# Attention then SwiGLU on one core: weights loaded between x and the last rows, and a new order of the opening steps

## The chip, the cores and the metric

The kernel runs on one core of a Trainium2 chip. The metric is the device time of one execution in microseconds (us); less is better. The core has five engines that run side by side, each through its own list of instructions in order: TensorE (PE, matrix products), VectorE (DVE), ScalarE (ACT), GpSimd (POOL) and SyncE (SP, which here only issues the DMA transfers). An instruction waits for semaphores of the instructions whose results it reads or whose buffers it overwrites, and whatever stands behind it on its engine waits too.

## The reference

```
def mab(q, kv):                              # x: 4 x 12416 x 128, inducing: 32 x 128
    s = scale * (q @ kv.transpose(0, 2, 1))
    s = s - s.max(-1, keepdims=True)
    a = np.exp(s)
    a /= a.sum(-1, keepdims=True) + 1e-09
    return a @ kv
h = mab(I, x)                                # 32 rows gather from all of x
y = mab(x, h)                                # each row of x reads the 32 rows of h
g = y @ w_gate                               # 128 x 1536
out = (g / (1 + np.exp(-g)) * (y @ w_val)) @ w_out   # 1536 x 128
```

The three weights arrive as 64-bit floats and x as 32-bit floats.

## The kernel before

A batch has 12416 rows; a "slot" is one of 12 slices of the hidden width (1536 = 12 x 128) for one tile of up to 512 rows, and a batch has 300 slots. In a slot PE makes a gate product and a value product (`front`, lines 694 and 695), ACT the silu (`gate`), DVE the product of both (`value`), ACT or DVE a rounded copy h_hi and POOL or DVE the rest h_lo (`split`), and PE adds three products with the output weights (`back`, lines 737 to 739). The attention of the next batch is woven into the slots. Only the first batch has nothing to be woven into, so the kernel opens with a prologue whose order is written out by hand in two tables of tokens, START and SECOND; the list of every engine follows the order of the tokens.

The prologue of batch 0 goes as follows. Seven chunks of x (14 blocks of 128 rows each, the last 13) are loaded with the channels on partitions. Each chunk gets scores (`s1`) and their maximum, an exponential (`e1`), a transposition of the exponentials on DVE (`eT`), and a sum over the rows weighted by them (`hq`, 2 PE rows per block). `hq` needs x with rows on partitions, which comes either from a second load (`ln`) or by turning blocks on PE with a copy out of PSUM on DVE or ACT (`tx`). Chunks 0 to 3 share one maximum and 4 to 6 another (`mb`); `hb` and `hc` join the two halves into h, and `hd` turns it (hT, hTs).

Each weight piece is 128 x 512 numbers of 64 bits, 512 KB: J0 to J5 for the gate and value weights (a piece serves two slots), o0 to o2 for the output weights (a piece serves four). It is converted to 32 bits by integer steps: `X` (scale the high words) and `low` (scale the low words) on ACT, `sh` and `jn` on DVE (lines 190 and 193), `add` on POOL (line 196). Then the J pieces are multiplied by hT (`pa`, line 402), because the gate product works on attention weights and not on y, and are rounded in ACT and DVE steps (`pk`, `pb`, `pm`, `pc`). The o pieces are split into wo_hi (`hi`, ACT) and wo_lo (`lo`, POOL).

The first tile of 512 rows is served in its own short way (`z0` to `z8`): scores against hTs, maximum, exponential, sum, division, and a spread into `stack`, which `front` reads. In SECOND `f`, `g`, `m`, `k` are front, silu, value and back of the 12 slots of this tile; `back` uses the 32-bit weights whole for it (`u.whole`, line 734). Slots 0 to 11 are this tile; slot 12 opens the loop, when seven of the tile's twelve backs are done and five are pending; the loop takes one back per slot.

```
if u.whole:
    k = t % (WP // P)
    nc.tensor.matmul(out=o[:, :n], lhsT=pieces[f"o{t // (WP // P)}"].w[:, P * k:P * k + P], rhs=u.h[:, :n], ...)
```

Of the kernel before, what the change touches and what calls it, by code (L numbers as in the profile page):

```python
# [9 lines left out]
F32 = mybir.dt.float32  # L10
# [8 lines left out]
P = 128  # L19
# [9 lines left out]
def starts(sizes):  # L29
# [46 lines left out]
low:o0 X:o0 sh:J2 X:J3 sb:4:20:0 z6:0 z7:0 jn:J2 pk:0 z6:1 z7:1 z8:0 pb:0 pa:1 z8:1 sh:o0 sh:J3 e2:4:20 add:J2 jn:o0 pk:1 f:0 pm:1 sl g:0 pc:1 f:1
jn:J3 pa:2 f:2 g:1 add:o0 m:0 pk:2 X:J4 sum:1 f:3 pm:2 add:J3 rec:1 m:1 g:2 X:o1 k:0 pa:3 pc:2 g:3 low:J4 sh:J4 m:2 f:4 f:5 jn:J4 k:1 pk:3 sh:o1 g:4
m:3 no:1:1 pm:3 k:2 at:1 X:J5 sh:J5 pc:3 g:5 low:J5 jn:J5 low:o1 jn:o1 add:J4 pa:4 add:J5 f:6 m:4 pk:4 m:5 g:6 pb:4 k:3 f:7 pa:5 m:6 add:o1 ah:1:1 f:8
al:1:0 g:7 X:o2 pk:5 sh:o2 g:8 low:o2 k:4 pm:5 f:9 jn:o2 pc:5 k:5 f:10 sp:1 m:7 k:6 m:8 f:11 g:9 add:o2 m:9 g:10 g:11 m:10 m:11 hi:o0 lo:o0 hi:o1
lo:o1  # L80
# [3 lines left out]
    13: "hi:o2",  # L84
    14: "lo:o2",
# [26 lines left out]
def induced_set_attention_then_swiglu(ctx: ExitStack, tc: tile.TileContext, xt, xn, ind, wgv, wo, out):  # L112
# [58 lines left out]
    class Piece:  # L171


        def __init__(self, work, k, i):
            self.k, self.i = k, i
# [7 lines left out]
        def low(self):  # L183
            nc.scalar.activation(out=self.lw.bitcast(I32), in_=self.lw, func=AF.Copy, scale=2.0 ** -29)  # L184
# [684 lines left out]
```

## Time and profile before

| what | value |
|---|---|
| runs (3) | 1376.89, 1376.9, 1377.32 us; median 1376.9 |
| span of the profiled execution, first to last instruction | 1374.8 us |
| PE busy in the span | 1366.1 us (99%) |
| ACT, DVE, POOL busy | 91%, 87%, 86% |
| DMA traffic | 119.49 MB, mean 87 GB/s |

The profile is of one execution. Its span is 2.1 us under the median of the runs, the part of a run that lies outside its first and last instruction. A busy share is a mean over stages: PE is bound from the loop on, while the prologue's 55 us have other limits, so the prologue is read by stages.

### The profile page before, as it was taken

The numbers are of one execution on the slowest core, as the hardware profiler recorded it, in microseconds if no ns is written. First come the engines' busy times: TensorE is split into PE (matmuls) and PEld (weight loads), VectorE is DVE, ScalarE is ACT, GpSimd is POOL, SyncE is SP. The second block draws the span as 40 slices with busy tenths as digits, with TensorE's granted clock in tenths as the row PEclk, the third lists the DMA queues.
The fourth block names the chain that finished last, engine by engine and source line by source line (L and its number), as shares of the span: only waits on it lengthen the run. The fifth ranks groups of instructions, "written<-read, shape, count | busy, mean of one in ns | idle before, by whom it ended". The sixth has DMA issues, their size and how long they took to land.

```text
span 1374.8 us, 25215 instructions
## 1 busy us (share of the span) xinstructions
PE 1366.1 (99%) x7459; PEld 1183.8 (86%) x7459; DVE 1195.4 (87%) x2088; ACT 1245.7 (91%) x2380; POOL 1179.8 (86%) x994
## 2 busy tenths in 40 slices
PE   9999999999999999999999999999999999999998
PEld 6578788889988887899998888789999888889998
DVE  6899879998988889898898888988888888888887
ACT  4989898889998887999999889799999999999998
POOL 1689878989988878899899878889989989989987
PEclk9999999999999999999999999999999999999999
DMA  9234433312144243221123522321111111111110
GB/s 370 81 96 133 160 104 114 119 56 71 38 130 160 94 143 112 67 62 37 44 72 119 192 80 95 123 73 52 44 38 45 39 47 39 39 46 38 43 44 22
DMA packets 50680, 119.49 MB, mean 87 GB/s; under 512 B 11376, under 2 KB 28272, under 8 KB 50544
## 3 DMA queue, kind: packets, MB, share of 16 engines
q1 hardware_dynamic: 50544, 117.90, 26.3%
q8 instruction: 59, 0.97, 0.3%
q14 instruction: 77, 0.63, 0.2%
HBM read 62.54 MB, written 25.43 MB: 64 GB/s over the span
## 4 chain that ended last, share of the span: by engine, by line
PE 97%; ACT 1%; DMA 1%; DVE 1%; issue 0%; SPq 0%; DVEq 0%
PE o L737 18%; PE gv L694 18%; PE gv L695 18%; PE o L738 18%; PE o L739 18%; PE gv L275 2%; PE o L323 1%; PE o L275 1%; DMA xt_sb<-xt 1%; PE o L734 0%; ACT silu L700 0%; PE gv L424 0%; PE gv L267 0%; ACT xn_sb L184 0%; DVE eT L313 0%
## 5 line engine op out<-in xcount | busy, mean ns | idle before, releaser
L718 POOL TENSOR_TENSOR h_lo<-h,h_hi 128x512 fp32r<-128x512 f32 (+1 forms) x889 | 1088.6, 1250 | 147.7 <-ACT h_hi L716 104.7
L700 ACT ACTIVATE silu<-gv 128x512 f32<-128x512 f32 (+1 forms) x1200 | 704.8, 589 | 95.5 <-PE gv L694 69.9
L708 DVE TENSOR_TENSOR h<-gv,silu 128x512 f32<-128x512 f32 (+1 forms) x891 | 590.9, 669 | 90.5 <-PE o L738 50.7
L716 ACT CAST h_hi<-h 128x512 fp32r<-128x512 f32 (+1 forms) x778 | 468.9, 603 | 0.8 <-DVE h L708 0.8
L694 PE MATMUL gv<-stack,tw 128*128 128x512 f32 (+1 forms) x1200 | 452.7, 377 | 1.3 <-DVE stack L544 1.0
L695 PE MATMUL gv<-stack,tw 128*128 128x512 f32 (+1 forms) x1200 | 448.2, 374 | 0.0
L737 PE MATMUL o<-h_hi,wo_lo 128*128 128x512 f32 (+1 forms) x1188 | 445.6, 375 | 0.0
L739 PE MATMUL o<-h_lo,wo_hi 128*128 128x512 f32 (+1 forms) x1188 | 443.2, 373 | 0.0
L738 PE MATMUL o<-h_hi,wo_hi 128*128 128x512 f32 (+1 forms) x1188 | 443.2, 373 | 0.0
L708 DVE TENSOR_TENSOR gv<-gv,silu 128x512 f32<-128x512 f32 (+1 forms) x297 | 201.5, 678 | 66.0 <-PE o L738 46.0
L694 PEld LDWEIGHTS gv<-stack,tw 128*128 128x128 f32 x1200 | 227.0, 189 | 33.9 <-ACT tw L416 3.0
L737 PEld LDWEIGHTS o<-h_hi,wo_lo 128*128 128x128 f32 x1188 | 224.8, 189 | 33.4 <-issue 10.6
L695 PEld LDWEIGHTS gv<-stack,tw 128*128 128x128 f32 x1200 | 227.0, 189 | 28.0 <-ACT silu L700 1.6
L739 PEld LDWEIGHTS o<-h_lo,wo_hi 128*128 128x128 f32 x1188 | 224.8, 189 | 24.3 <-POOL h_lo L718 0.3
L738 PEld LDWEIGHTS o<-h_hi,wo_hi 128*128 128x128 f32 x1188 | 224.8, 189 | 23.2
L718 DVE TENSOR_TENSOR h_lo<-gv,h_hi 128x512 fp32r<-128x512 f32 (+1 forms) x297 | 197.6, 665 | 0.8
L716 ACT CAST h_hi<-gv 128x512 fp32r<-128x512 f32 (+1 forms) x295 | 168.8, 572 | 10.1 <-DVE gv L708 8.4
L211 DVE TENSOR_REDUCE h_hi<-h 128x512 fp32r<-128x512 f32 (+1 forms) x113 | 73.7, 661 | 0.0
L748 DVE COPY ob<-o 128x512 f32<-128x512 f32 (+1 forms) x99 | 65.8, 665 | 0.2 <-PE o L739 0.2
L484 POOL TENSOR_TENSOR a_lo<-aT,a_hi 128x480 fp32r<-128x480 f32 (+2 forms) x26 | 29.9, 1151 | 0.0
L196 POOL TENSOR_TENSOR wgv_sb<-s_all 128x512 int32<-128x512 int32 x2 | 2.9, 1487 | 28.4 <-ACT s_all L184 28.4
L471 POOL TENSOR_TENSOR s_all<-s_all,sm 128x512 f32<-128x512 f32 (+2 forms) x27 | 26.1, 966 | 0.0
(156 smaller groups left out, 480.2 us busy)
## 6 DMA issues: line engine op xcount, KB each, us to landing
xt_sb<-xt SPq DMA_DIRECT2D x32, 896.0 KB, 5.1
xn_sb<-xn SPq DMA_DIRECT2D x18, 896.0 KB, 6.1
out<-ob SPq DMA_DIRECT2D x52, 256.0 KB, 2.0
out<-ob SPq DMA_DIRECT2D x48, 240.0 KB, 2.0
stack<-a_hi SPq DMA_DIRECT2D x96, 64.0 KB, 2.0
stack<-a_lo SPq DMA_DIRECT2D x96, 64.0 KB, 2.0
stack<-a_hi SPq DMA_DIRECT2D x96, 60.0 KB, 2.0
stack<-a_lo SPq DMA_DIRECT2D x96, 60.0 KB, 2.0
```

Source lines behind the costliest of these rows:

```text
L211: nc.vector.tensor_reduce(out=out, in_=in_.unsqueeze(2), op=ALU.max, axis=AX.X)
L275: nc.tensor.matmul(out=ps[32 * j:32 * j + 32, 32 * (lo - b0):32 * (hi - b0)], lhsT=lhsT, rhs=st.xt[q][:, lo - CH0[q]:hi - CH0[q], j, :], s ...
L694: nc.tensor.matmul(out=u.g[:, :n], lhsT=st.w[:, wcol(0, t)], rhs=rhs, start=True, stop=True)
L695: nc.tensor.matmul(out=u.v[:, :n], lhsT=st.w[:, wcol(1, t)], rhs=rhs, start=True, stop=True)
L700: nc.scalar.activation(out=u.s[:, :u.n], in_=u.g[:, :u.n], func=AF.Silu)
L708: nc.vector.tensor_mul(out=u.h[:, :n], in0=u.v[:, :n], in1=u.s[:, :n])
L716: u.cast(out=u.hi[:, :n], in_=u.h[:, :n])
L718: eng.tensor_sub(out=u.lo[:, :n], in0=u.h[:, :n], in1=u.hi[:, :n].bitcast(F32))
L737: nc.tensor.matmul(out=o[:, :n], lhsT=wo_lo[:, ws], rhs=hi, start=(t == 0), stop=False)
L738: nc.tensor.matmul(out=o[:, :n], lhsT=wo_hi[:, ws], rhs=hi, start=False, stop=False)
L739: nc.tensor.matmul(out=o[:, :n], lhsT=wo_hi[:, ws], rhs=lo, start=False, stop=(t == NT - 1))
L748: (nc.scalar.copy if u.last else nc.vector.tensor_copy)(out=ob[:, :n], in_=o[:, :n])
```

## The change

Both tables are written anew, and steps that were one token are parted so that PE's half and the reader's half can stand apart (`tp`/`te`, `s1p`/`s1e`, `mbp`/`mbe`, `ha0`/`hap`/`har`, `hdp`/`hds`/`hdt`, `fg`/`fv`).

- Loads: the chunks of x come in the order 0, 3, 2, 1, 5, 4, 6; then J1, o1, o0, J3, J2, J0; then the rows of chunk 6; then J4, J5, o2. Chunks 0 to 5 are turned on PE whole (84 blocks; before 61, with chunks 4, 5 and two thirds of 6 loaded a second time).
- Weights are joined in place: `t` of a J piece is its place in wgv_sb. `X` and `low` of J1, o1, o0 and `X` of J3 and o2, `low` of J5, run on POOL. Six of the nine pieces have their `sh`, and five their `jn`, ahead of `hc`.
- The first tile takes the split weights like all others (three fp32r products per back; `u.whole` is gone), so its h is split too, its first ten casts (`c`) and ten remainders (`l`) in SECOND.
- `pm` and `pc` go for all pieces; the first tile's scores use the layout of the others with a DVE transposition (`z0t`); four groups of PE transposes whose result is not used (`wm`, 5 + 5 + 3 + 10 blocks behind the first 9) go; `hi` and `lo` of o2 move from slots 13 and 14 into the first tile.

```
-lx:0:0:4 lx:0:4:14 lx:1 lx:2 lx:3 lx:4 lx:5 lx:6 ln:4 ln:5 ln:6:0:8 ld:J0:s0 ld:J1:s1 ld:J2:t0 ld:J3:t1 wm:9
+lx:0:0:4 lx:0:4:14 lx:3 wm:9 tp:0:0 te:0:0:1 lx:2 tp:0:1 tp:0:3 te:0:1:0 s1p:0 te:0:3:1 tp:0:2 s1e:0 lx:1 ...
-            self.t = work[:, 2 * WP:3 * WP].bitcast(U32)
             self.w = work[:, 2 * WP:3 * WP] if k == "o" else wgv_sb[:, self.cs]
+            self.t = self.w.bitcast(U32)
...
-        def X(self):
-            nc.scalar.activation(out=self.t.bitcast(F32), in_=self.hw.bitcast(F32), func=AF.Copy, scale=2.0 ** -112)
+        def X(self, e=0):
+            if e:
+                nc.gpsimd.tensor_scalar(out=self.t.bitcast(F32), in0=self.hw.bitcast(F32), scalar1=2.0 ** -112, scalar2=None, op0=ALU.mult)
+            else:
+                nc.scalar.activation(out=self.t.bitcast(F32), in_=self.hw.bitcast(F32), func=AF.Copy, scale=2.0 ** -112)
...
-        if u.whole:
-            k = t % (WP // P)
-            nc.tensor.matmul(out=o[:, :n], lhsT=pieces[f"o{t // (WP // P)}"].w[:, P * k:P * k + P], rhs=u.h[:, :n], start=(t == 0), stop=(t == NT - 1))
-        else:
-            hi, lo = turns(u.hi[:, :n]), turns(u.lo[:, :n])
...
+        hi, lo = turns(u.hi[:, :n]), turns(u.lo[:, :n])
+        nc.tensor.matmul(out=o[:, :n], lhsT=wo_lo[:, ws], rhs=hi, start=(t == 0), stop=False)
+        nc.tensor.matmul(out=o[:, :n], lhsT=wo_hi[:, ws], rhs=hi, start=False, stop=False)
+        nc.tensor.matmul(out=o[:, :n], lhsT=wo_hi[:, ws], rhs=lo, start=False, stop=(t == NT - 1))
```

**DVE, the last steps ahead of `hc`.** Before, between the second maximum and `hc` (L384), DVE has the transpositions eT and small steps of the join alone:

```order
L313 STREAM_TRANSPOSE eT<-s_all 128x448 x2
L313 STREAM_TRANSPOSE eT<-s_all 128x416
L354 TENSOR_REDUCE fac<-sum_262 128x1
L357 TENSOR_TENSOR fac<-fac 128x2
L361 TENSOR_REDUCE r_445<-gv 128x1
L362 TENSOR_SCALAR r_445<-r_445 128x1
L363 RECIPROCAL r_445<-r_445 128x1
L364 TENSOR_SCALAR fac<-fac,r_445 128x2
L381 TENSOR_SCALAR hn<-o,fac 128x128
L384 SCALAR_TENSOR_TENSOR hn<-o,fac,hn 128x128
```

In the changed kernel the same stretch (here from the second half's `ha0` on, L381; `hc` is L416, `sh` L196, `jn` L199) reads:

```order
L381 TENSOR_TENSOR fac<-fac 128x2
L196 TENSOR_SCALAR wgv_sb<-wgv_sb 128x512
L331 STREAM_TRANSPOSE eT<-s_all 128x448
L389 TENSOR_REDUCE r_456<-gv 128x1
L390 TENSOR_SCALAR r_456<-r_456 128x1
L391 RECIPROCAL r_456<-r_456 128x1
L392 TENSOR_SCALAR fac<-fac,r_456 128x2
L196 TENSOR_SCALAR wgv_sb<-wgv_sb 128x512
L413 TENSOR_SCALAR hn<-o,fac 128x128
L331 STREAM_TRANSPOSE eT<-s_all 128x416
L199 SCALAR_TENSOR_TENSOR wgv_sb<-tw,wgv_sb 128x512 x2
L196 TENSOR_SCALAR wgv_sb<-wgv_sb 128x512
```

Weight steps now stand between the small ones, and two `jn` and a `sh` between the last eT and `hc`, which is the next row. Three more `sh` and three `jn` stand ahead of this piece.

**POOL, its first work after the constants.** Before it is the adds, from J0 on:

```order
L196 TENSOR_TENSOR wgv_sb<-s_all 128x512 x2
L196 TENSOR_TENSOR wgv_sb<-tw 128x512
L196 TENSOR_TENSOR xn_sb<-xn_sb 128x512
L196 TENSOR_TENSOR wgv_sb<-tw 128x512
L471 TENSOR_TENSOR s_all<-s_all,sm 128x512
```

In the changed kernel seven steps with one tensor input, `X` (L191) and `low` (L185) of J1, o1, o0 and `X` of J3, stand ahead of the first add (L202):

```order
L191 TENSOR_SCALAR wgv_sb<-tw 128x512
L185 TENSOR_SCALAR tw<-tw 128x512
L191 TENSOR_SCALAR s_all<-s_all 128x512
L185 TENSOR_SCALAR s_all<-s_all 128x512
L191 TENSOR_SCALAR s_all<-s_all 128x512
L185 TENSOR_SCALAR s_all<-s_all 128x512
L191 TENSOR_SCALAR wgv_sb<-tw 128x512
L202 TENSOR_TENSOR s_all<-s_all 128x512
L202 TENSOR_TENSOR wgv_sb<-wgv_sb,tw 128x512
L202 TENSOR_TENSOR s_all<-s_all 128x512
```

The DVE step `sh` of a piece waits for its `X`, so DVE's list now depends on POOL's ahead of `hc`.

**PE, the end of the first tile.** Before, a front (L694, L695) and a whole back (L734, two passes of 512 columns):

```order
L694 MATMUL gv<-stack,tw 128x512
L695 MATMUL gv<-stack,tw 128x512
L734 MATMUL o<-h_hi,s_all 128x512
L694 MATMUL gv<-stack,tw 128x512
L695 MATMUL gv<-stack,tw 128x512
```

In the changed kernel the back has three rows of one pass each:

```order
L743 MATMUL gv<-stack,tw 128x512
L738 MATMUL gv<-stack,tw 128x512
L787 MATMUL o<-h_hi,wo_lo 128x512
L788 MATMUL o<-h_hi,wo_hi 128x512
L789 MATMUL o<-h_lo,wo_hi 128x512
```

The gate product (L738) of the next slot now goes ahead of a back and its value product (L743) behind it.

## Rows read from the trace of the kernel before

**Rows 1.** The page: busy time by engine, and the chain by engine.

```profile
PE 1366.1 (99%) x7459; PEld 1183.8 (86%) x7459; DVE 1195.4 (87%) x2088; ACT 1245.7 (91%) x2380; POOL 1179.8 (86%) x994
...
PE 97%; ACT 1%; DMA 1%; DVE 1%; issue 0%; SPq 0%; DVEq 0%
```

**Rows 2.** Windows: stretch: length, busy time (instructions) by engine, granted clock, DMA, GB/s.

```profile
20.90:28.00 7.10, 6.72 (x164) 5.41 (x155) 5.31 (x20) 2.89 (x8) 0.00 (x0) 1.00 1.01 406
28.00:36.80 8.80, 7.34 (x76) 4.48 (x75) 7.99 (x21) 7.91 (x18) 4.22 (x3) 1.00 0.94 343
36.80:54.74 17.94, 17.05 (x50) 8.89 (x51) 16.08 (x29) 17.04 (x31) 9.15 (x7) 1.00 0.10 27
```

**Rows 3.** The chain that ended last, 48 to 66 us: start, length, what.

```profile
54.91 0.22 PE gv L694
...
55.34 0.86 PE o L734 x2
...
61.36 0.22 PE gv L694
...
62.87 0.22 PE gv L694
...
63.30 0.22 PE o L737
...
63.95 0.22 PE gv L694
```

**Rows 4.** Timeline, 19 to 28.9 us: start, length, instruction, idle time before it.

```profile
19.39 0.54 PE L275 MATMUL gv<-xt,indT 128*32 128x416 f32 x2
20.61 0.55 DVE L285 TENSOR_SCALAR_CACHE_REDUCE s_all<-gv 128x416 f32<-128x416 f32 x1
...
26.27 1.06 PE L375 MATMUL o<-xn,eT 128*32 128x128 f32 x26
27.34 0.68 ACT L187 ACTIVATE s_all<-s_all 128x512 f32<-128x512 f32 x1 [2.79 <-DMA s_all<-wgv]
27.68 0.35 DVE L384 SCALAR_TENSOR_TENSOR hn<-o,fac,hn 128x128 f32<-128x128 f32 x1
```

**Rows 5.** Timeline: prices of the steps on DVE.

```profile
22.21 0.64 DVE L313 STREAM_TRANSPOSE eT<-s_all 128x448 f32<-128x448 f32 x1
28.72 0.42 DVE L190 TENSOR_SCALAR s_all<-s_all 128x512 uint32<-128x512 uint32 x1
29.17 0.69 DVE L193 SCALAR_TENSOR_TENSOR s_all<-s_all 128x512 uint32<-128x512 uint32 x1
51.74 1.28 DVE L708 TENSOR_TENSOR h_hi<-gv,silu 128x512 f32<-128x512 f32 x2
```

**Rows 6.** Groups on POOL, 0 to 60 us: count, busy us, mean ns.

```profile
L196 POOL TENSOR_TENSOR wgv_sb<-s_all 128x512 int32<-128x512 int32 x2 | 2.9, 1487 | 28.4 <-ACT s_all L184 28.4
L196 POOL TENSOR_TENSOR wgv_sb<-tw 128x512 int32<-128x512 int32 x2 | 2.6, 1290 | 1.8 <-ACT stack L541 1.8
masks.py:199 POOL TENSOR_SCALAR_AFFINE_SELECT ident<-ident 128x128 f32<-128x128 f32 x1 | 0.3, 292 | 0.1
masks.py:197 POOL MEMSET ident<- 128x128 f32 x1 | 0.2, 204 | 0.0
L142 POOL MEMSET odd<- 128x1 f32 x1 | 0.1, 98 | 0.0
```

**Rows 7.** Timeline, 28 to 55 us: the first front, the load of tile 1.

```profile
36.80 0.48 PE L694 MATMUL gv<-stack,tw 128*128 128x512 f32 x1 [1.02 <-DVE stack L544]
49.91 0.68 DVE L484 TENSOR_TENSOR a_lo<-aT,a_hi 128x512 fp32r<-128x512 f32 x1
51.82 0.58 SPq L500 DMA_DIRECT2D stack<-a_lo  x1
```

**Rows 8.** DMA issues, 0 to 70 us: count, KB each, us from issue to landing.

```profile
xn<-xn SPq DMA_DIRECT2D x2, 896.0 KB, 18.0
...
stack<-a_lo SPq DMA_DIRECT2D x6, 64.0 KB, 2.0
```

More of the change, by code (lines that the diff above doesn't have):

```diff
@@ L76 @@
[L76 to L79, printed above, removed]
@@ L505, in z0, with z0t @@
             st.zps = psum()
[L506 to L507 removed]
+            scores(st.hTs, 0, FC[0], st.zps)
+        def z0t():
+            st.z = sgl.tile([P, FC[0], M], F32, name="z")
+            nc.vector.transpose(out=st.z.rearrange("p t m -> p (t m)"), in_=st.zps[:, :M * FC[0]])
         def z1():
             st.zm = att.tile([P, FC[0]], F32, name="zm")
[L511 removed]
+            nc.vector.tensor_reduce(out=st.zm, in_=st.z, op=ALU.max, axis=AX.X)
         def z2():
[L514 to L516 removed]
+            nc.vector.tensor_sub(out=st.z, in0=st.z, in1=st.zm.unsqueeze(2).broadcast_to([P, FC[0], M]))
         def z3():
@@ L682, in induced_set_attention_then_swiglu, with front_g, front_v, front @@
         last = near = False
-    def front(st, b, c, t):
+        hi = lo = None
+        cast = nc.scalar.copy
+        due = NT
+    def front_g(st, b, c, t):
         u = Tile()
         q, j = COLS[c]
-        u.b, u.q, u.j, u.t = b, q, j, t
+        u.b, u.q, u.j, u.t, u.st = b, q, j, t, st
         n = u.n = WF if q == 0 else 32 * FC[q]
-        u.whole = b == 0 and c == 0
-        rhs = turns(st.stack[c][:, :n])
+        u.rhs = turns(st.stack[c][:, :n])
         u.g = ps_gv.tile([P, 512], F32, name="gv")
+        nc.tensor.matmul(out=u.g[:, :n], lhsT=st.w[:, wcol(0, t)], rhs=u.rhs, start=True, stop=True)
+        return u
+    def front_v(u):
         u.v = ps_gv.tile([P, 512], F32, name="gv")
-        nc.tensor.matmul(out=u.g[:, :n], lhsT=st.w[:, wcol(0, t)], rhs=rhs, start=True, stop=True)
-        nc.tensor.matmul(out=u.v[:, :n], lhsT=st.w[:, wcol(1, t)], rhs=rhs, start=True, stop=True)
+        nc.tensor.matmul(out=u.v[:, :u.n], lhsT=u.st.w[:, wcol(1, u.t)], rhs=u.rhs, start=True, stop=True)
+    def front(st, b, c, t):
+        u = front_g(st, b, c, t)
+        front_v(u)
         return u
@@ L756, in first, with cast @@
     def first(t):
-        made.append(front(cur, 0, 0, t))
+        made.append(front_g(cur, 0, 0, t))
         pend.append(made[t])
-    short |= dict(f=first, g=lambda t: gate(made[t]), m=lambda t: value(made[t]), k=lambda t: back(pend.pop(0)))
+    def cast(t, e):
+        made[t].cast = (nc.scalar.copy, same)[e]
+        high(made[t])
+    short |= dict(fg=first, fv=lambda t: front_v(made[t]), g=lambda t: gate(made[t]), m=lambda t: value(made[t]),
+                  c=cast, l=lambda t: low(made[t]), k=lambda t: back(pend.pop(0)))
     for token in SECOND.split():
         run(token)
+    wait += [u for u in made if u.lo is None]
     cur.steps = [(slot, lambda token=token: run(token)) for slot, tokens in FIRST.items() for token in tokens.split()]
@@ L861 @@
         blk = o[:, P * NG * 32 * c0:P * NG * 32 * (c0 + c)].reshape(B, -1, P, n)
-        backs = [turn if c0 == 0 and b == 0 else turn[turn] for b in range(B)]
-        blk = np.stack([x[..., np.argsort(k)] for x, k in zip(blk, backs)])
+        blk = blk[..., np.argsort(turn[turn])]
         if c0 == 0:
```

204 lines of the change are left out of this document (115 added, 89 removed).

## The prediction

> **What bounds the kernel now.** I read the page first: PE is busy 99% of the span and carries 97% of the chain that ended last [rows 1]. So the loop costs what PE's products cost, and a change of the prologue counts by how much sooner or later PE can run the loop's products without a gap. Next came the windows by stage [rows 2]. From 28.0 to 36.8 us DVE is busy 7.99 of 8.80 and ACT 7.91: the first tile's scores and the first weights share them. From 36.80 to 54.74 ACT is busy 17.04 of 17.94 with 31 instructions (0.55 us each), PE could do its products in less, and this stage ends when ACT and DVE have served twelve slots. The chain then shows PE without a gap: slot 12 opens at 54.91, and slot 17 at 61.36, since each of the five slots takes a front (2 x 0.215) and one whole back of 0.86, 1.29 in all; a slot with a split back takes 1.08 (62.87 to 63.95) [rows 3]. Slot 17 is my finishing line: from there both kernels do the same work, and 61.36 stands against 1376.9.
>
> The prologue's own marks are: the last chunk of x has its scores started at 19.39; `hc`, the last step of h, is at 27.68; J0 is in at 27.34 [rows 4]; the first front is at 36.80 [rows 7].
>
> **The change, part by part.**
>
> *Loads.* The chunks of x end where they did, near 19.39. Behind them stood, up to J0, 2 x 0.917 MB of rows, 0.524 of chunk 6's and 0.524 of J0 [rows 8]: 2.88 MB, at the 406 GB/s of that stretch [rows 2] 7.1 us, so 26.5; J0 came at 27.34, 0.84 late. Now six pieces (3.15 MB) and chunk 6's rows (0.85 MB) stand there, 4.0 MB or 9.85 us: those rows land at 29.2, with the same lateness at 30.1. The last `hq` waits for them and takes 1.06 [rows 4]: `hc` at 31.1 at best, 30.3 without lateness. Less is loaded in all (the rows of chunks 4 and 5), but that saving lies behind `hc`'s wait, in J4, J5 and o2, which nobody is yet waiting for. The 23 more turned blocks are PE work of some 2.5 us while PE waits for loads anyway, and their copies lie on ACT ahead of 28.5; I cost them at nothing. If that cover went they would push the last `hq`, by 2.5.
>
> *DVE and POOL ahead of `hc`.* DVE has read chunk 6's scores at 21.2 [rows 4]. From there its list holds, up to `hc`, six `sh` at 0.40 (0.42 long), five `jn` at 0.62 (0.69 long, spaced as two products that took 1.28 together), three eT at 0.6 and small steps of 1.7 [rows 5]: 2.4 + 3.1 + 1.8 + 1.7 = 9.0, so 30.2 if it never waited. It waits for POOL. J1 lands near 21.3 (19.39, 1.3 for 0.524 MB, some lateness), and POOL then does seven steps with one input. The trace of before has none of that size. The nearest is the affine select of 128 columns, 0.292 long, where a start alone costs 0.098: 0.0015 per column, so 0.87 for 512. The lower end is the memset (0.204 for 128 columns: 0.52), the upper the two-input add (1.29) [rows 6]. I take 0.87, the only row with an input and an output. Then `X` of o1 ends at 23.9, of o0 at 25.65, of J3 at 27.4, and DVE runs: `sh` J1 22.2 to 22.6, the maximum, `jn` J1 to 23.5, `sh` o1 at 23.9, `jn` o1 to 25.0, `sh` o0 at 25.7, eT and `jn` o0 to 27.3, `sh` J3 at 27.5, eT to 28.5, the sum's four small steps to 29.3, `sh` J2 and `hb` to 30.0, eT to 30.6, two `jn` and a `sh` to 32.25, `hc` at 32.3. Queued behind the first wait are the second maximum and with it the exponentials of chunks 4 to 6, and behind all of it h. With 0.52 it is 31.6, with 1.29 it is 35.2. So `hc` is 4.6 us later than before (bounds +2.6, by the loads, and +7.5).
>
> By the Trainium skill (GPSIMD Engine Reference, section 3.1), a loop over 512 elements with one input was measured at 769 ns; no run here shows it yet, and by that figure `hc` would be at 32.1.
>
> *`hc` to the first front.* Before 9.12 (27.68 to 36.80). Now the same tile steps stand in DVE's list with `jn` J0, both steps of J4 and J5 and two `pb`: 0.75 of waits (for the scores against hTs above all) and 8.3 of steps by the same prices end in the two `stack` writes at 9.1 behind `hc`. DVE's list is as long as before, so I take no gain (bounds -0.75 and, with as much waiting again, +0.75). POOL's adds of J1, J3 and J0 end at 35.1; the tile's last PE step, which stands behind their products, has its input at 38.5, so they are hidden, and cost what they end after that.
>
> *The first tile.* Now five of six `sh`/`jn` pairs are gone from it, as are all four `pm`/`pc`; added are ten casts on ACT, three remainders on DVE and seven on POOL, and the steps of o2. DVE's list from the first front up to the remainder of tile 1's attention (`al`, which the load of slot 12's rows waits for) is eight products, four `pb`, two remainders, `jn` and `al` (sixteen at 0.62), and sum, `sh` and a transposition (1.9): 11.8. From the end of `al` (50.59) to the landing of its last load (issued at 51.82, 2.0 to land: 53.8) it is 3.2 [rows 7, 8]. That gives slot 12 at 14.95 behind the first front, against 54.91 - 36.80 = 18.1. ACT's list is as long: 27 instructions of 0.55 are 14.85. Two engines both full wait for each other; before, ACT in this stage reached 95%. At 95% the stage takes 15.7 to 15.8, and I take 0.9 for it and the first slots behind it, where two casts and two remainders (POOL's at 1.28) are still due. Gain 3.15 less 0.9; bounds 3.15 and 0.
>
> *The five split backs in the loop.* Five slots of 1.08 for five of 1.29: 5.4 for 6.45, a gain of 1.05. `hi` and `lo` of o2 leave slots 13 and 14, where PE set the pace: nothing; if ACT set it there, 0.55.
>
> *Sum.* +4.6 - 0 - 3.15 + 0.9 - 1.05 = +1.3. Slot 17 at 62.7, span 1376.1, time **1378.2 us**, 0.1% up. Under 0.2% (2.75 us) this kernel's measurement can hardly tell a difference, so I call it the same.
>
> **Rivals.**
>
> *POOL's one-input steps cost what its adds cost.* For: each runs while DVE reads two inputs, and adds beside such steps took 1.487 where others took 1.290 [rows 6]. Against: one input less. At 1.29, `hc` is at 35.2 and the time 1381.1. It decides from 1.08 on, where `hc` is 1.45 later and the time passes 1379.65. **17%**, slower.
>
> *Contention alone.* The same rows as a factor of 1.15 on POOL, and 0.07 on each `jn` by DVE: POOL's step at 1.0 puts `hc` at 33.2 with 0.35 more for `jn`; 1379.4, still within 0.2%. By the Trainium skill (GPSIMD Engine Reference, section 1, Specifications) POOL shares its SBUF interfaces with VectorE and contends with DVE instructions that have two SBUF inputs; the two pairs of rows agree. **10%**, the same.
>
> *The split tile is no shorter.* ACT and DVE alternate: a silu, a product, a cast and a remainder of a slot follow one another over three engines, and only six PSUM buffers carry slots (`ps_gv`). If the twelve slots take the old 18.1, the time is 1380.4 + 0.7 for POOL's late remainders, 1381.1. For: ACT's 95% before came with less to wait for. **15%**, slower.
>
> *The clock falls.* The granted clock is 1.00 in all three windows [rows 2], in which PE was kept at work by `wm`. Without it PE has gaps of about 1.6 us, between the last but one and the last `hq` and ahead of hTs. At the lower level (1.2 GHz) the PE steps from `hc` to the first front, some 1.9 us, double: 1380.1; if the first tile ran so too, its 12 us of products would take 24 and the time pass 1385. By the Trainium skill (TensorE: Matmul & The Clock Gate, Part 1) the throttled clock is the default and activity releases it; by that rule taking out `wm` would cost. **6%**, slower.
>
> *DVE is not held.* If the rows land at 29.2, the small POOL price holds and DVE's list closes up, `hc` is at 30.3, and a first tile at the bound of 14.95 gives 1375.3; with slots at PE's own pace (12 x 1.08 = 13.0) 1373.4. For: the older prologue kept ACT 95% busy, so waits can be small. Against: 9.0 us of DVE steps must fit into 9.1. **14%** for a time under 1374.15.
>
> **How the numbers follow.** The forecast itself has 38%, with contention alone 48% for "same". Slower holds 17 + 15 + 6 = 38%, faster 14%. The range runs from 1374.4 (leaving out about one in ten below) to 1383.0 (above it lie a lasting lower clock and two slow cases at once).
>
> **What would show it.** Right: `hc` (its L416 on DVE) at 31.5 to 33, with the idle time ahead of `sh` put down to POOL L191; chunk 6's rows landing near 30; 9 us from `hc` to the first L738; slot 12's L738 some 15 to 16 us behind it; slots of 1.08 at once. Wrong: POOL's L191 above 1.08 or below 0.6; a granted clock under 1.00 between 28 and 60; slot 12 more than 17 or less than 14 behind the first front; or any difference behind slot 17, where I expect none.

## The result, and the profile after

The changed kernel takes 1393.14 us (median of 4 runs, 1392.06 to 1395.11) against 1377.11 for the kernel before: 1.0117 times as long, 95% interval 1.0103 to 1.0132. I had forecast 1378.2, the same time, and a range up to 1383.0. It is slower by 16 us, clear of the noise and outside the range.

The page of the changed kernel (busy time by engine, chain by engine, as [rows 1]) still shows a loop that PE bounds; it says nothing of the loss:

```profile
PE 1368.2 (98%) x7467; PEld 1187.4 (85%) x7467; DVE 1207.0 (87%) x2092; ACT 1248.7 (90%) x2389; POOL 1205.7 (87%) x1012
...
PE 95%; DVE 0%; ACT 0%; issue 0%
```

The marks of the prediction do. All are starts in the profiled executions, whose spans are 1374.8 and 1390.2:

| mark | before | forecast | after |
|---|---|---|---|
| chunk 6's scores read (DVE) | 20.61 | 20.6 | 21.97 |
| `hc` | 27.68 | 32.3 | 40.66 |
| first front | 36.80 (+9.12) | +9.1 | 53.20 (+12.54) |
| slot 12 | 54.91 (+18.11) | +15.85, with the 0.9 | 70.70 (+17.50) |
| slot 17 | 61.36 (+6.45) | +5.4 | 76.33 (+5.63) |
| from there to the end | 1313.4 | the same | 1313.9 |

(Slots by the chain, as in [rows 3].) So `hc` takes 13.0 of the 15.4 us by which the spans differ, the stretch from `hc` to the first front 3.4, the tile and the five slots give back 1.4, and the other 0.4 comes at the very end, behind the issue of the last output (1386.86 against 1371.96, 14.90 later). In the loop between, both kernels do the same work in the same time. The windows by stage (PE, PEld, DVE, ACT, POOL; granted clock; DMA share; GB/s), to be read against [rows 2]:

```profile
28.00:40.66 12.66, 6.73 (x112) 5.37 (x112) 9.34 (x16) 6.06 (x11) 11.74 (x9) 0.76 0.34 133
40.66:53.20 12.54, 8.26 (x66) 3.86 (x66) 11.00 (x22) 6.41 (x13) 9.85 (x8) 0.83 0.00 1
53.20:70.70 17.50, 13.60 (x50) 8.79 (x50) 17.16 (x27) 14.19 (x27) 12.32 (x10) 1.00 0.07 18
```

Ahead of `hc` POOL is the full engine (11.74 of 12.66), where it had nothing to do before. In the tile DVE is (17.16 of 17.50). The groups of the weight steps, 20 to 53 us (busy us, mean ns, idle time before):

```profile
L202 POOL TENSOR_TENSOR wgv_sb<-wgv_sb,tw 128x512 int32<-128x512 int32 x6 | 8.5, 1420 | 3.3 <-DVE wgv_sb L199 2.0 <-issue 1.3
L196 DVE TENSOR_SCALAR wgv_sb<-wgv_sb 128x512 uint32<-128x512 uint32 x6 | 7.7, 1287 | 1.8 <-POOL wgv_sb L191 1.8
L185 POOL TENSOR_SCALAR s_all<-s_all 128x512 int32<-128x512 uint32 x2 | 3.6, 1796 | 0.2
L191 POOL TENSOR_SCALAR wgv_sb<-tw 128x512 f32<-128x512 f32 x2 | 3.1, 1540 | 19.2 <-DMA tw<-wgv 19.1
L196 DVE TENSOR_SCALAR s_all<-s_all 128x512 uint32<-128x512 uint32 x2 | 0.9, 427 | 3.5 <-POOL s_all L191 3.5
```

Two prices stand out. POOL's scalings ahead of `hc` cost 1.52 to 1.80, not 0.87. And `sh` (L196), 0.42 in [rows 5], has a mean of 1.287 in one of its two groups and 0.427 in the other. The timeline of DVE and POOL ahead of `hc` shows why (start, length, instruction, idle time before it):

```profile
24.32 1.54 POOL L191 TENSOR_SCALAR s_all<-s_all 128x512 f32<-128x512 f32 x1
25.90 0.43 DVE L196 TENSOR_SCALAR s_all<-s_all 128x512 uint32<-128x512 uint32 x1 [1.62 <-POOL s_all L191]
25.95 1.80 POOL L185 TENSOR_SCALAR s_all<-s_all 128x512 int32<-128x512 uint32 x1
...
29.38 0.43 DVE L196 TENSOR_SCALAR s_all<-s_all 128x512 uint32<-128x512 uint32 x1 [1.86 <-POOL s_all L191]
...
32.78 1.28 POOL L202 TENSOR_TENSOR s_all<-s_all 128x512 int32<-128x512 int32 x1
32.84 1.50 DVE L196 TENSOR_SCALAR wgv_sb<-wgv_sb 128x512 uint32<-128x512 uint32 x1 [1.84 <-POOL wgv_sb L191]
...
35.46 1.29 POOL L202 TENSOR_TENSOR s_all<-s_all 128x512 int32<-128x512 int32 x1
35.50 1.53 DVE L196 TENSOR_SCALAR wgv_sb<-wgv_sb 128x512 uint32<-128x512 uint32 x1
...
38.80 1.66 POOL L202 TENSOR_TENSOR wgv_sb<-wgv_sb,tw 128x512 int32<-128x512 int32 x1 [0.56 <-DVE wgv_sb L199]
39.24 1.50 DVE L196 TENSOR_SCALAR wgv_sb<-wgv_sb 128x512 uint32<-128x512 uint32 x1
40.66 0.34 DVE L416 SCALAR_TENSOR_TENSOR hn<-o,fac,hn 128x128 f32<-128x128 f32 x1
```

The waits put down to L191 (1.62, 1.86, 1.84) are those that I had looked for, only larger. The long `sh` are not in a wait: they are shown as running, and each ends 0.28 behind the POOL add that had started just ahead of it (32.78 + 1.28 = 34.06, and 32.84 + 1.50 = 34.34).

The clock fell, too: 0.76 and 0.83 in the two windows up to 53.20.

### The profile page after: what moved, and what is told of

Its sections match the earlier page's. It is cut to its first block, busy times and chain, and to the rows that moved or that the text cites. A ratio compares the mean times of both kernels' runs of the same rounds, so it can differ in the third digit from the quotient of the medians.

```text
span 1390.2 us, 25254 instructions
## 1 busy us (share of the span) xinstructions
PE 1368.2 (98%) x7467; PEld 1187.4 (85%) x7467; DVE 1207.0 (87%) x2092; ACT 1248.7 (90%) x2389; POOL 1205.7 (87%) x1012
## 4 chain that ended last, share of the span: by engine, by line
PE 95%; DVE 0%; ACT 0%; issue 0%
PE o L787 18%; PE gv L738 18%; PE o L789 18%; PE o L788 18%; PE gv L743 18%; PE gv L282 2%; PE o L341 1%; PE o L282 1%; PE gv L465 0%; ACT silu L752 0%; DVE h_lo L767 0%; DVE h L757 0%; PE gv L349 0%; DVE wo_lo L208 0%; PE o L420 0%
## 5 line engine op out<-in xcount | busy, mean ns | idle before, releaser
L767 POOL TENSOR_TENSOR h_lo<-h,h_hi 128x512 fp32r<-128x512 f32 (+1 forms) x898 | 1100.3, 1253 | 153.4 <-ACT h_hi L761 109.8
L761 ACT CAST h_hi<-h 128x512 fp32r<-128x512 f32 (+1 forms) x787 | 474.1, 603 | 2.1 <-DVE h L757 1.9
L738 PE MATMUL gv<-stack,tw 128*128 128x512 f32 (+1 forms) x1200 | 448.9, 374 | 5.6 <-DVE h_lo L767 2.8
L743 PE MATMUL gv<-stack,tw 128*128 128x512 f32 (+1 forms) x1200 | 449.0, 374 | 0.3 <-DVE tw L450 0.2
L738 PEld LDWEIGHTS gv<-stack,tw 128*128 128x128 f32 x1200 | 226.7, 189 | 36.0 <-DVE h_lo L767 3.6
L743 PEld LDWEIGHTS gv<-stack,tw 128*128 128x128 f32 x1200 | 226.7, 189 | 28.0 <-ACT silu L752 2.1
L191 POOL TENSOR_SCALAR wgv_sb<-tw 128x512 f32<-128x512 f32 x2 | 3.1, 1540 | 19.2 <-DMA tw<-wgv 19.1
```

The source lines that it names most:

```text
L738: nc.tensor.matmul(out=u.g[:, :n], lhsT=st.w[:, wcol(0, t)], rhs=u.rhs, start=True, stop=True)
L743: nc.tensor.matmul(out=u.v[:, :u.n], lhsT=u.st.w[:, wcol(1, u.t)], rhs=u.rhs, start=True, stop=True)
L761: u.cast(out=u.hi[:, :u.n], in_=u.h[:, :u.n])
L767: eng.tensor_sub(out=u.lo[:, :n], in0=u.h[:, :n], in1=u.hi[:, :n].bitcast(F32))
```

## The experiments

Theories: **P**, the price of POOL's scalings, for which DVE waits; **H**, DVE steps held up by POOL steps that run beside them; **C**, the lower clock; **L**, loads and turned blocks; and for the stretches behind `hc`, a wait for a buffer and DVE's list in the tile. A table behind the runs gives the marks of all.

**e1: scalings on ACT.**

```diff
-X:J1:1 ... low:J1:1 ... X:o1:1 ... low:o1:1 ... X:o0:1 ... low:o0:1 ... X:J3:1 ... X:o2:1 ... low:J5:1
+X:J1 ... low:J1 ... X:o1 ... low:o1 ... X:o0 ... low:o0 ... X:J3 ... X:o2 ... low:J5
```

> The changed kernel with all nine X and low steps that it gave to POOL put back on ACT, same places in the order. Price theory (POOL takes 1.5 to 1.8 us for such a step, and DVE sat idle 5.3 us ahead of hc waiting for it): hc goes from 40.7 to 34 to 36, the time from 1393.1 to 1384 to 1387. Port theory alone (DVE's sh is held up by any POOL step, the adds too): the adds still hold it, hc at 38 to 39.5, time 1390 to 1392. Clock theory alone: the gaps of PE stay, time within 1 us of 1393.

1388.7 us, `hc` at 36.53, between what the two theories forecast. `hc` is 4.1 us sooner and the time 4.4 shorter; counted from chunk 6's scores, which came 1.1 sooner in this execution, `hc` gains 3.0. That is P, set against what DVE now waits for ACT (3.4 in all ahead of `hc`, where it had waited 5.3 for POOL). Two `sh` beside POOL's adds still took 1.15 and 1.51, so H is left.

**e2: `sh` in another form.**

```diff
-tensor_scalar(out=self.t, in0=self.t, scalar1=3, scalar2=0x7FFFFFF8, op0=ALU.logical_shift_left, op1=ALU.bitwise_and)
+scalar_tensor_tensor(out=self.t, in0=self.t, scalar=3, in1=mask.broadcast_to([P, WP]), op0=..., op1=...)
```

> The changed kernel with DVE's sh written as a step with a second input (the mask, one column broadcast), so that it runs at one column per cycle: 0.69 us instead of 0.42 when nothing is in its way. Port theory (sh took 1.5 us where a POOL step ran): sh takes 0.7 everywhere, hc 2 us earlier, the first front 3 to 4 us earlier, time 1389 to 1390.5. Price theory: DVE still waits for POOL's steps, sh costs 0.27 more each, time 1393 to 1395.

1394.96 us, `hc` at 42.12. The form with a second SBUF tensor is held up as well: 1.78 where an add had started 0.07 ahead, 0.69 where none ran. Neither forecast came true as it stood: changing the form is no way out.

**e4: PE kept busy.** Dummy transposes ahead of `ha0`, the last `hq`, `hc` and pa:0.

```diff
-... tp:5:1 ha0 ... low:J0 hq:6 ... sh:J0 hc ... z2 pa:0
+... tp:5:1 wm:34 ha0 ... low:J0 wm:34 hq:6 ... sh:J0 wm:30 hc ... z2 wm:16 pa:0
```

> The changed kernel with PE transposes whose result is not used in four places (34 ahead of the small fold product, 34 ahead of the last hq, 30 behind it, 16 ahead of the first weight product). Clock theory (the granted clock was 0.50 to 0.85 from 30 to 36 and from 38 to 46): the clock is 1.00 throughout, the last hq takes 1.1 and not 1.8, the products behind hTs 2 us less, time 2 to 4 us less: 1389 to 1391. Price and port theories: DVE's list sets the pace, time within 1 us of 1393.

1395.35 us. The granted clock was 1.00 from 25 to 55 us, and `hc` at 40.91: C does not delay `hc`. The third group, 30 blocks, stood ahead of the product that reads what `hc` writes, and DVE waited 2.7 for that product, so this run says nothing on the stretch that follows.

**e5: the kernel before without its `wm`.**

```diff
-tx:0:0 wm:5 s1:0 ... X:J0 wm:5 hd wm:3 sh:J0 ... sM:4:20 wm:10 z2
+tx:0:0 s1:0 ... X:J0 hd sh:J0 ... sM:4:20 z2
```

> The kernel before without its four later groups of PE transposes whose result is not used (5, 5, 3 and 10 blocks). Theory A (they keep the granted clock up and the changed kernel pays for their loss): the granted clock falls under 1.00 somewhere between 20 and 37 us and the time is 1 to 3 us longer. Theory B (PE's own work is enough in that order): clock 1.00, time within 0.5 us of the kernel before.

1379.1 us, ratio 1.0011 (1.0002 to 1.0021). The granted clock (the last number but two) fell to the lower of its two levels, 1.2 GHz (0.50), behind `hc`, where PE had been busy 1.19 of 2.00:

```profile
28.00:30.00 2.00, 1.19 (x24) 0.73 (x15) 1.21 (x6) 0.00 (x0) 0.00 (x0) 1.00 1.02 403
...
32.00:34.00 2.00, 2.00 (x17) 0.79 (x10) 1.04 (x4) 1.90 (x5) 2.00 (x2) 0.50 0.52 201
34.00:37.00 3.00, 2.82 (x26) 1.16 (x29) 2.93 (x9) 1.97 (x4) 0.71 (x1) 0.50 0.83 221
```

`hc` to the first front took 10.22 for 9.12 (that `hc` itself was 1.4 later goes with chunk 6's scores, 21.99 for 20.61). By the ratio `wm` was worth 1.5 us in the kernel before (0.3 to 2.9); that is the size of C there.

**e6: load buffers of J2 and J0 swapped**, so that the three pieces whose space the first `pk` takes over are J1, J3 and J0.

```diff
-ld:J2:t2 ... ld:J0:u0
+ld:J2:u0 ... ld:J0:t2
```

> The changed kernel with J2 and J0 in each other's load buffers. The rounded weights st.w take over the buffer of three pieces; the first pk (ACT) waited 3.0 us until the add of J2, the last of the three, at 48.9. If that wait counts: pk can start when its product is there (about 46), the first front is 1 to 2 us earlier, time 1391 to 1392. If not (z6 waits for DVE until 49.0 anyway): the time stays within 0.5 us of 1393.1.

1392.62 us, in all the same. But the stretch from `hc` to the first front is 10.87 for 12.54. In the changed kernel `pk` had waited for the add of J2, the last reader of that space; with the swap it waits for PE alone:

```profile
47.02 0.59 ACT L446 CAST tw<-gv 128x512 fp32r<-128x512 f32 x1 [0.65 <-PE gv L443]
```

against, in the changed kernel,

```profile
48.92 1.56 ACT L446 CAST tw<-gv 128x512 fp32r<-128x512 f32 x3 [3.00 <-POOL wgv_sb L202]
```

The 1.7 that the stretch gained is not this wait alone, since the hold-ups in it fell otherwise in this execution (z5 took 0.28 instead of 1.36, `jn` of J5 1.72 instead of 0.69). What it gave was lost at both ends: `hc` came 1.1 later, and slots 12 to 16 ran partly at the lower clock (7.16 for 5.47, below).

**e8: as e1, adds of J1, o1, o0 and the remainder of o1 moved behind `hc`** in the order of the tokens.

```diff
-... jn:o0 add:o1 ... add:J1 har ... hi:o1 hb add:o0 ... lo:o1 jn:J2 hi:o0
+... jn:o0 ... har ... hb ... jn:J2
+X:J4 add:J1 jn:J0 add:J3 ...
```

> The changed kernel with all nine POOL scalings on ACT (as in e1) and with the four POOL steps that stood ahead of `hc` (three adds, one remainder, with the two casts that read them) moved behind it, so that POOL does nothing while DVE goes through `sh` and `jn`. Theory A (a POOL step that has started holds a DVE `sh` or `jn` up until it ends): every `sh` ahead of `hc` at 0.42 and every `jn` at 0.69, where e1 showed 1.15, 1.51 and pairs of `jn` at 1.94; `hc` about 2 to 3 us sooner than in e1's 36.5, near 34. Theory B (the long `sh` come from something else, such as the place that they write): `sh` stays at 1.1 to 1.5 in places and `hc` stays near 36.5. The adds come later, so the time can be 1386 to 1390 by either.

1387.5 us, `hc` at 35.17. The move only half did what it said: POOL's list was shorter ahead of `hc`, but its adds started as soon as their `jn` was done, at 24.46 and 33.35. Just the two `sh` beside those two took 1.30 and 1.52; the four others took 0.42 or 0.43. The clock was 1.00 from 25 to 75 us, and this execution (1386.15) was still 9 us slower than the kernel before: C is not the loss.

**e9: scalings as they were, the six `sh` and five `jn` that stood ahead of `hc`, with what follows from them, put behind it.**

```diff
-... low:J1:1 sh:J1 ... mbe:1 jn:J1 X:o1:1 ... sh:o1 ... jn:o1 ... sh:J0 hc
+... low:J1:1 ... mbe:1 X:o1:1 ... hc
+... z0t sh:J1 jn:J1 add:J1 X:J5 sh:J0 jn:J0 add:J0 z1 ...
```

> The changed kernel with its POOL and ACT steps where they are, but with the six `sh` and five `jn` (and the adds, casts and the remainder that follow them) taken from ahead of `hc` and put behind it. Theory A (the weight steps in DVE's list, through their waits for POOL and the hold-ups, make `hc` late): `hc` at the bound that the loads set, 30.3 to 31.5, some 9 to 10 us sooner than in the changed kernel; the 7 us of steps come back behind `hc`, so the time falls by 2 to 6 us, to 1387 to 1391. Theory B (chunk 6's rows, the 23 more turned blocks or the lower clock make it late): `hc` at 36 or later.

`hc` at 31.34: the bound of the loads, as forecast. The last `hq` waits for chunk 6's rows alone, which let it start at 30.27 (30.1 in the prediction):

```profile
30.27 1.03 PE L406 MATMUL o<-xn,eT 128*32 128x128 f32 x26 [0.90 <-DMA xn<-xn]
31.34 0.35 DVE L416 SCALAR_TENSOR_TENSOR hn<-o,fac,hn 128x128 f32<-128x128 f32 x1 [2.58 <-PE o L406]
```

So L is 3.7 us of the 13, and the DVE steps ahead of `hc`, with what they wait for, the other 9.3. I had expected the time to fall to 1387 to 1391; it rose, to 1395.85: the steps were done behind `hc` with PE idle and at the lower clock (0.50 in 40 to 45 and in 55 to 60 us), and the tile took 24.6.

**e10: `sh` and `jn` of o2 from the tile to the place where DVE waited 1.06 for `pk`.**

```diff
-sh:J5 z5 pb:0 ... g:5 sh:o2 fv:5 ... c:5:0 jn:o2 fv:7
+sh:J5 z5 sh:o2 jn:o2 pb:0 ... g:5 fv:5 ... c:5:0 fv:7
```

> The changed kernel with `sh` and `jn` of o2 moved from the first tile to the place behind z5 where DVE waits for the first `pk` (1.06 idle). Theory A (the first tile lasts as long as DVE's list, 17.16 busy of 17.50): first front to slot 12 falls by what these two took in the tile, 1.6 us, to about 15.9, and the time by 1.2 to 1.6. Theory B (the tile is set by the chain over ACT, DVE and PSUM buffers): no change, within 0.4 us.

1391.28 us. The tile took 15.88, where I expected 15.9, for 17.50. It is shorter by what the two steps had taken in it (0.51 and 1.11), although the granted clock was 0.83 in it, and DVE is still the engine with the most work (PE, PEld, DVE, ACT, POOL; granted clock; DMA share; GB/s):

```profile
55.31:71.19 15.88, 14.48 (x50) 10.65 (x50) 14.76 (x23) 14.04 (x27) 11.92 (x10) 0.83 0.08 20
```

So the tile's length follows DVE's list.

**e7: prices by themselves.** Test steps ahead of the kernel before.

```diff
+nc.gpsimd.tensor_scalar(out=qe, in0=qb, scalar1=2.0, ...)                    # 512, and 256 columns
+nc.gpsimd.tensor_scalar(out=qe, in0=raw2[:, :, 1], scalar1=2.0, ...)         # words 8 bytes apart
+nc.gpsimd.tensor_add(out=qc, in0=qb, in1=qb)
```

> The kernel before with a group of test steps ahead of its own work, on the space of the weights, which is written later; they compute nothing that is used and its whole time says nothing. POOL alone: scaling of 512 and of 256 contiguous columns, of 512 high words that stand 8 bytes apart, of 512 low words with integer conversion; then eleven adds in a row, beside which DVE does twice each a product of two tensors, `sh`, `jn`, a maximum, a transposition and a copy. Theory A (each element that POOL scales costs what the traces show, 1.5 to 1.6 us for 512, wherever it stands): 512 contiguous at 1.4 to 1.6, 256 at about 0.8. Theory B (the distance of 8 bytes makes it dear): 512 contiguous at 0.8 to 0.9 as I priced it, 8 bytes apart at 1.5. For DVE, theory A (a POOL step holds up those DVE steps that read two tensors from SBUF or run `sh`): product, `sh` and `jn` stretched to end 0.2 to 0.3 behind a POOL add, maximum and transposition at 0.67 and 0.7; theory B (all contend alike): all stretched by the same share.

Its own rows on POOL (L172: 512 contiguous, L174: 256, L176: 8 bytes apart, L178: an add; a row of x2 holds the 0.08 between its two steps):

```profile
5.12 1.49 POOL L172 TENSOR_SCALAR wgv_sb<-wgv_sb 128x512 f32<-128x512 f32 x1
6.58 1.04 POOL L178 TENSOR_TENSOR wgv_sb<-wgv_sb 128x512 f32<-128x512 f32 x1
...
9.15 1.90 POOL L174 TENSOR_SCALAR wgv_sb<-wgv_sb 128x256 f32<-128x256 f32 x2
11.14 3.19 POOL L176 TENSOR_SCALAR wgv_sb<-wgv_sb 128x512 f32<-128x512 f32 x2
```

The distance is not what makes a scaling dear (1.49 against 1.52 and 1.59): it is POOL's price for a scaling, 0.85 and 0.97 for 256 columns and 1.49 for 512. An add of two tensors (1.04) is cheaper than a scaling of one. DVE did not meet the adds as intended, and no `sh` of this run ran beside one. The second `sh` began 0.71 behind the start of a scaling and took its usual 0.41; the first began 1.19 behind one's start and took 0.65. So a scaling can hold an `sh` up, but not through its whole length, as an add does. A maximum and a transposition beside adds took 0.68 and 0.70, their usual time.

**e12: the add of J0 first of the adds.** Its `jn` stands behind `hc`, and POOL's list is in order, so no add can run ahead of `hc`; the scalings stay on POOL. (The adds and the remainder leave START as in e8.)

```diff
+X:J4 jn:J0 add:J0 add:J1 add:J3 hdp ...
```

> The changed kernel with its POOL scalings as they are, but the add of J0, whose `jn` stands behind `hc`, put first of the adds in POOL's list, so that no POOL step with two inputs can run ahead of `hc` (the adds of J1, o1, o0 and the remainder of o1 come behind it). Theory A (a two-input POOL step holds a DVE `sh` or `jn` up until 0.28 or 0.55 behind its own end, a one-input step hardly does): every `sh` ahead of `hc` at 0.42, `jn` at 0.65 to 0.69, and `hc` 3.2 to 4 us sooner, at 36.7 to 37.5, with the waits for POOL's scalings (5.3 us) still there. Theory B (it is the scalings that hold DVE up, or the waits for them absorb it): `hc` within 1 us of 40.7. The adds come late, so I expect no gain of time beyond 3 us by either.

```profile
29.35 0.43 DVE L196 TENSOR_SCALAR s_all<-s_all 128x512 uint32<-128x512 uint32 x1 [1.87 <-POOL s_all L191]
...
32.87 0.43 DVE L196 TENSOR_SCALAR wgv_sb<-wgv_sb 128x512 uint32<-128x512 uint32 x1 [1.89 <-POOL wgv_sb L191]
...
36.74 0.42 DVE L196 TENSOR_SCALAR wgv_sb<-wgv_sb 128x512 uint32<-128x512 uint32 x1
37.08 0.35 DVE L416 SCALAR_TENSOR_TENSOR hn<-o,fac,hn 128x128 f32<-128x128 f32 x1
```

All `sh` ahead of `hc` take 0.41 to 0.43, all `jn` under 0.7, and `hc` is at 37.08: H is 3.6 us, with P's waits as they were. The time, 1392.62, did not fall, since the adds are late now, and `pk` with them:

```profile
48.45 1.56 ACT L446 CAST tw<-gv 128x512 fp32r<-128x512 f32 x3 [6.57 <-POOL wgv_sb L202]
```

**e13: the same, with the scalings on ACT.**

> As e8 (all scalings on ACT), with the add of J0 first of the adds, so that POOL runs nothing of the weights ahead of `hc`. Theory A (hold-ups and waits for POOL add up): the two long `sh` of e8 (1.30 and 1.52) at 0.42, and `hc` 2.0 us sooner than e8's 35.2, near 33.2, the rest up to e9's 31.3 being DVE's own list and ACT. Theory B (they lie beside waits for ACT): `hc` within 0.6 us of 35.2.

1386.67 us, the shortest of these, though not clearly below e8 (1386.10 to 1387.81 against 1386.15 to 1388.08). Every `sh` ahead of `hc` takes 0.42 or 0.43, but `hc` is at 35.58. Chunk 6's scores came late in this execution (23.61); counted from them `hc` is 1.1 sooner than in e8, not 2.0, because a wait for ACT grew from 0.49 to 1.36: ACT is now busy without a gap (11.50 of the 11.50 us up to `hc`).

**e11: four mends together** (e8, e6, e10, and for pieces 2 to 5 `pm` and `pc` in place of `pb`).

> The changed kernel with four mends together: scalings on ACT and adds of J1, o1, o0 later in POOL's list (as in e8), J2 and J0 with swapped load buffers (as in e6), `sh` and `jn` of o2 sooner (as in e10), and for the pieces 2 to 5 the rest of the attention weights by a PE product and an ACT copy (`pm`, `pc`, as before the change) in place of a DVE subtraction of 0.69. Theory A (the loss is the sum of DVE's list, its hold-ups and the wait for the shared buffer, and each mend keeps its worth): `hc` near 35, 10.5 to 11 to the first front, a first tile of 14.5 to 16, and a time of 1380 to 1384. Theory B (what one mend gives is lost at the next wait): 1386 to 1389, as e8 alone.

1389.37 us: slower than e8 alone. The wait for the shared buffer went, but `sh` and `jn` of o2 now met POOL's adds and took 1.52 and 1.67, and in the tile PE waited for ACT's `pk` and ACT for PE's `pm`, so the tile took 18.77 with DVE idle. What one mend gave, the next wait took.

The marks of all kernels (us; slot 12 by the start of its gate product, and slots 12 to 16 together; in the first two rows both by the chain, as in the table of the marks above):

| kernel | chunk 6 read | `hc` behind it | to first front | to slot 12 | 12 to 16 |
|---|---|---|---|---|---|
| before | 20.61 | 7.07 | 9.12 | 18.1 | 6.45 |
| e5, without `wm` | 21.99 | 7.06 | 10.22 | 18.4 | 6.45 |
| e9, no `sh`, `jn` ahead | 21.38 | 9.96 | 17.09 | 24.6 | 7.2 |
| e13, POOL empty ahead | 23.61 | 11.97 | 12.91 | 17.7 | 5.5 |
| e8 | 22.10 | 13.07 | 12.08 | 17.7 | 5.5 |
| e11, four mends | 22.39 | 13.06 | 13.72 | 18.8 | 5.5 |
| e12, scalings on POOL, no adds | 22.20 | 14.88 | 16.05 | 18.0 | 5.5 |
| e1, adds on POOL, no scalings | 20.82 | 15.71 | 11.60 | 17.5 | 7.2 |
| after | 21.97 | 18.70 | 12.54 | 17.5 | 5.5 |
| e4, PE kept busy | 21.86 | 19.05 | 13.73 | 17.5 | 7.2 |
| e2, other `sh` | 21.40 | 20.72 | 13.09 | 17.8 | 5.5 |
| e6, buffers swapped | 21.02 | 20.75 | 10.87 | 17.5 | 7.2 |
| e10, o2 sooner | 21.15 | 20.80 | 13.35 | 15.9 | 5.5 |

In e6 and e10 the scores came sooner than in the changed kernel and `X` of J1 began later (21.86 and 22.06 for 20.97), so DVE waited 2 us more for `X`. The changed kernel, e4, e6 and e10 have the same DVE and POOL steps ahead of `hc`, and it lies at 40.66 to 41.95, or 18.7 to 20.8 behind the scores: one execution of a kernel tells such a mark to 1 or 2 us, and differences smaller than that are not shown by this table.

## Why the prediction failed, step by step

Three of the signs that it named for being wrong came: L191 above 1.08, a granted clock under 1.00 between 28 and 60 us, and slot 12 more than 17 us behind the first front.

**Loads: right.** Chunk 6's rows let the last `hq` start at 30.27, and with nothing else in the way (e9) `hc` is at 31.34 against "31.1 at best".

**DVE and POOL ahead of `hc`: this step failed**, by 8.4 us (32.3 forecast, 40.66 measured), at two places. The list was well counted: from the end of the scores' read (22.55) to 40.66 it is 18.1, less 5.3 of waits and 4.4 of hold-ups 8.4, where I had 9.0. The scores were read 1.4 later than I had them; in the table this varies by as much and more from one kernel to the next.
- *The price.* I priced a scaling at 0.87, "the only row with an input and an output", a select of 128 columns, and took the two-input add (1.29) for the upper end, since it has one input more. Measured: 1.52 to 1.80, above that end. DVE waits 5.3 (1.62, 1.86, 1.84) instead of 2.1. My rival with 1.29 was on the right side and too small. The Trainium skill (GPSIMD Engine Reference, section 3.1) gives 769 ns for a tight loop over 512 elements (it names no number of inputs there, only a higher floor for two); this kernel's scaling takes twice that, and the measurement decides.
- *The hold-ups.* I read the two groups of adds in [rows 6], 1,487 against 1,290, as contention, a factor of 1.15. The mean hid what it was. Of the two adds behind the 1,487, one took 1.29, like the others, and the other 1.68; that one had begun 0.17 behind a `jn`:

```profile
30.24 0.69 DVE L193 SCALAR_TENSOR_TENSOR s_all<-s_all 128x512 uint32<-128x512 uint32 x1
30.41 1.68 POOL L196 TENSOR_TENSOR wgv_sb<-s_all 128x512 int32<-128x512 int32 x1 [28.38 <-ACT s_all L184]
```

So the add seems to have stood still for 0.39 of the 0.52 us for which that `jn` still ran. The trace of before showed it for POOL behind DVE, and the change made it happen to DVE behind POOL. In the kernel before, an `sh` could cost 0.42 because only one began while an add ran, 0.11 ahead of its end (0.43); the rows from which I took the price, at 28.72 and 29.17 in [rows 5], stand ahead of POOL's first add. Here three `sh` run beside one (3.3 us lost), and with a `jn`, an `sh` at a scaling's start and a small step it is 4.4; e12 gets 3.6 to 3.8 of it back. The Trainium skill (SBUF — State Buffer, section "Who interferes with whom") states it: VectorE and GpSimd share a pair of ports, an exclusive lock for the whole instruction, and whoever starts first makes the other wait. The rows agree for adds: 1.28 and 1.50 with ends 0.28 apart. For scalings they do not: an `sh` that began 0.67 behind the start of one took 0.41 (e12), and the measurement decides. I had cited that they share interfaces, and priced the rule as a factor of 1.15 on POOL and 0.07 a `jn` instead of as a whole instruction.

Taken apart by the runs, from chunk 6's scores to `hc`: before 7.1; loads and turned blocks +2.9 (e9); the DVE steps themselves and a full ACT +2.0 (e13); scalings on POOL in place of ACT +2.9 (e12); adds beside `sh` and `jn` +3.8 (after, 18.7). By the spread of the four kernels above each term is good to 1 or 2 us, so that P and H both count is shown, and which is the larger is not.

**`hc` to the first front: failed, by 3.4.** "DVE's list is as long as before, so I take no gain" left out that `pk` writes over the space of three loaded pieces, so that it waits for the add of J2 (3.00 of idle time on ACT, 1.06 on DVE behind it; in e6 that wait for the add is gone and the stretch 1.7 us shorter, not all of it by this), and that `sh`, `jn` and z5 are held up there too, by 2.95 in all.

**The first tile: right in mechanism, mis-sized.** It gave 0.6 of the 2.25 that I had forecast. DVE's list sets it. The last rows of the chain ahead of slot 12 are DVE's, with 0.3 of issue between them:

```profile
67.29 0.68 DVE h L757
67.97 0.61 DVE gv L757
68.58 0.79 DVE wo_lo L208
69.37 0.35 DVE h L757
69.72 0.17 issue
69.89 0.69 DVE h_lo L767
70.58 0.12 issue
70.70 0.45 PE gv L738
```

Up to the end of `al` the list took 14.2 (53.20 to 67.36), not 11.8. Fourteen of the sixteen steps took 0.67 each instead of 0.62, since some do not follow each other closely (9.4); `al` (1.44 long) and `jn` of o2 (1.11), which ran beside POOL's remainders, took 2.5 instead of 1.2; the sum, `sh` and the transposition 2.3 instead of 1.9. From the end of `al` to slot 12 it is 3.3, where I had 3.2: the load that I counted was issued at 68.59 and, with 2.0 to land, was there at about 70.6, as DVE's last step was. (11.8 and 3.2 are 15.0, where the prediction has 14.95; nothing hangs on it.) With o2's steps elsewhere (e10) the tile took 15.88, as much as I had forecast with them in it; that the two numbers meet is chance.

**Five split backs: right** (1.08 a slot from the second on), 0.8 gained for 1.05.

**The clock: a rival that came true and mattered little.** It fell twice ahead of the first front, each time behind a PE wait (3.75 us ahead of 31.06, 1.85 ahead of 37.87), but DVE was what PE waited for, and with the clock at 1.00 up to the first front `hc` gained nothing in e4, and e8 was 9 us slower than the kernel before all the same. It costs where PE sets the pace: behind the wait of 2.8 us ahead of slot 12 some executions run on at the lower level and take 7.16 for slots 12 to 16 instead of 5.47 (e1, e4, e6, e9).

**Not settled:** what order would keep the mends. e8 has `hc` 5.5 sooner and gains 5.6; e12 has it 3.6 sooner and gains 0.5, e11 5.2 and gains 3.8. The waits named with each run stand where the rest went, but no order without them was found, and none of these kernels beats the one before.

## What to carry to other kernels

Before a step moves to GpSimd, look in the trace for the DVE steps that will run beside it, not only for those that wait for it: in these runs DVE steps with two SBUF tensors, and the shift used here, stood still until a GpSimd add that began first was done, and were shown as busy. A price for an operation that the trace does not hold has no upper end in an operation that looks dearer; measure it, or let the range say that it is open. When a wait is mended, read what stands next in each engine's list, since the gain ends there.

## What was not expected of the hardware

- A GpSimd scaling of 512 columns (1.49 to 1.59 alone) costs more than its float add of two tensors (1.04) or its integer add (1.28).
- Beside GpSimd steps with two inputs, all 35 `sh` that began behind such a step's start and more than 0.1 us ahead of its end, in the changed kernel and nine built on it, ended 0.28 or 0.29 us behind its end; `jn` ended 0.55 to 0.68 behind it.
- Beside a scaling it depends on when the `sh` begins. Two that began 0.10 and 0.14 behind the scaling's start took 0.86 and 0.81; six that began 0.64 to 0.74 behind it took their usual 0.40 or 0.41; two that began 1.16 and 1.19 behind it took 0.68 and 0.65. `jn` that began 0.42 to 0.47 behind it took 0.91 to 1.06, later ones their usual 0.65 to 0.69, save two in e2 (0.92 and 1.03, begun 0.74 and 0.71 behind) whose scalings had themselves been held up (2.0 and 2.1). So a scaling seems to keep DVE out near its start and near its end, and not between; why was not tried.
- The hold-up goes both ways: the add at 38.80 took 1.66 instead of 1.28, since a `jn` had begun 0.16 ahead of it.
